# Token groups of two chunks behind the first, one v scaling moved ahead of other loads, and mix before score in the natural stops of a retention and snake kernel

## The chip, the cores and the metric

The kernel runs on one core of one Trainium2 chip. The metric is the device time of one execution in microseconds (us). Engines are named as the profile names them: PE is TensorE's matmul stream and PEld its weight loads, DVE is VectorE, ACT is ScalarE, POOL is GpSimd, SP is SyncE, which here only issues DMAs.

## The reference

Two layers follow each other. The first is a retention recurrence over 4 sequences of 768 tokens, with 8 heads of 64; its output, 3072 tokens of 512, goes into a feed-forward layer with a snake activation.

```python
for t in range(S):
    state = gamma[None, :, None, None] * state + np.einsum('bhd,bhe->bhde', k[:, :, t], v[:, :, t])
    y[:, :, t] = scale * np.einsum('bhd,bhde->bhe', q[:, :, t], state)
...
h = x @ w_in                                  # x: 3072 x 512, w_in: 512 x 2048
s = np.sin(alpha * h)
g = h + s * s / (alpha + 1e-09)
return (g @ w_out).astype(np.float32)         # w_out: 2048 x 512
```

## The kernel before

**Chunks and groups.** Each sequence is cut into six chunks of 128 tokens, 24 in all (`NJ`). The list `order`, also called `P`, holds first the four chunks 0 of the four sequences (`e0` to `e3`) and then, sequence by sequence, the chunks 1 to 5: `P[4]` to `P[8]` are of sequence 0, `P[9]` to `P[13]` of sequence 1, `P[14]` to `P[18]` of sequence 2, `P[19]` to `P[23]` of sequence 3. The list `sizes` (L49) cuts `P` into token groups for the feed-forward layer: 4, 2, 2, 2, 3, 3, 4, 4 chunks. Groups are numbered from 0.

**Attention of a chunk** has two parts. The score part multiplies keys with queries into PSUM (`pa`); DVE masks this into `aT`. The mix part multiplies `aT` with the scaled values and the state `s_bd` with the queries into `py`; DVE scales this into the chunk's columns of `xT`, the input of the feed-forward layer. It also adds keys times values of the chunk to the state, and casts of ACT, or of POOL for the last sequence, hand the state on as `s_bd` (L286, L391). Chunks of sequence 0 and `P[9]` take the natural form, `stage_A` for the score and `stage_M` for the mix. All later chunks are "wide" (L86) and take `scores`, `inter` and `mix`, which `burst` (L398) issues at one stop: state part of the old chunk, score of the new one, mix of the old one. DVE's and ACT's part of a burst follows at the next slot ("exit", "keep", "hand").

**Values and keys.** POOL issues all the loads that cast to bf16: `load_chunk` (L83, one DMA each for q, k and v of a chunk) and `load_seq` (L103, eight DMAs, one per head, for q, k or v of the wide chunks of a sequence). `scale_v` (L137) multiplies a chunk's values by a decay table on POOL, between these DMA issues, in program order. Queries and keys of a chunk are turned by DMA transposes that SP issues in order (`turn`, L256), or on PE at the start (`stage_T`).

**The feed-forward layer of a group** is a phase (L543). A phase goes through the 16 blocks of `d_ff`. `nf` blocks make a slot: 1 for groups of three and four chunks, 2 for groups of two, so that a slot has 512 columns of PSUM at most. In a slot PE makes `ph` (L425, four matmuls per block over all columns of the group), ACT takes the sine of each block (L428), squares the slot (L433; in the slots listed in `on_vector` DVE squares it, L435), and DVE adds (L440) into `gT`. While the phase of group g runs, PE also makes the output `po` of group g-1 (L450, 16 matmuls of 512 columns per chunk), spread over the slots; ACT copies a finished `po` to `o_sb` (L462) and SP stores it (L463). After the last phase PE makes the outputs of the last group with nothing beside them, the last chunk's in three column pieces (`last_tile`, L465).

**PSUM.** `ph` and `po` share the four buffers of tag "mm". A new `ph` waits until the buffer's last user is read: the adds of an earlier slot, or the copy of a finished `po`.

**Where attention stands.** `where` (L708 to L713) gives for each n the phase and slot after whose `ph` the stop for `P[n]` is made: there `P[n]` is scored and `P[n-1]` is mixed, the DMA transpose of `P[n+2]` is issued, and from n = 19 on `P[n]`'s values are scaled. All chunks of group g+1 must be mixed in the phase of group g. In a natural stop the score of `P[n]` is issued first and the mix of `P[n-1]` after it (L736 to L740).

**The start.** Group 0 is done by hand, up to L707, beside the weight loads. The loads of L670 to L697 are POOL's stream from then on.

Of the kernel before, what the change touches and what calls it, by code (L numbers as in the profile page):

```python
# [15 lines left out]
def kernel(  # L16
# [15 lines left out]
    nc = tc.nc  # L32
# [13 lines left out]

    order = [b * NCH for b in range(B)]
    order += [b * NCH + c for b in range(B) for c in range(1, NCH)]
    sizes = [4, 2, 2, 2, 3, 3, 4, 4]  # L49
    assert sum(sizes) == NJ  # L50
    NG = len(sizes)
    groups = [order[sum(sizes[:g]):sum(sizes[:g + 1])] for g in range(NG)]
# [16 lines left out]
    def chunk_of(t, j):  # L69
        b, c = divmod(j, NCH)  # L70
        return t[b, :, c * C:(c + 1) * C, :].rearrange("h s d -> s h d")

    def load_chunk(j, names="qkv"):
        for name, src in (("q", q), ("k", k), ("v", v)):
            if name not in names:
                continue
            if name == "v":
                t = big.tile([128, H, D], BF16, name="vr", tag="vr", bufs=10)
            else:
                if ("qk", j) not in raw:  # L80
                    raw["qk", j] = big.tile([128, 2, H, D], BF16, name="qkr", tag="qkr", bufs=9)
                t = raw["qk", j][:, "qk".index(name)]
            nc.gpsimd.dma_start(out=t, in_=chunk_of(src, j))  # L83
            raw[name, j] = t

    def wide(j):  # L86
        return j >= NCH + 2 and j % NCH > 0

    def load_seq(bt, names="qkv"):

        cs = [c for c in range(NCH) if wide(bt * NCH + c)]
        nh = 2 * len(cs)
        if "q" in names:
            raw["seq", bt] = (big.tile([128, nh, 2, NP, D], BF16, name=f"qk_seq{bt}"),
                              big.tile([128, nh, NP, D], BF16, name=f"v_seq{bt}"))
        tqk, tv = raw["seq", bt]
        for name, src in (("q", q), ("k", k), ("v", v)):
            if name not in names:
                continue
            for h in range(H):  # L100
                r = slice(64 * (h // NP), 64 * (h // NP) + 64)
                o = tv[r, :, h % NP, :] if name == "v" else tqk[r, :, "qk".index(name), h % NP, :]
                nc.gpsimd.dma_start(out=o, in_=src[bt, h, cs[0] * C:, :].rearrange("(f i) d -> i f d", i=64))  # L103
        for i, c in enumerate(cs):
            j, f = bt * NCH + c, slice(2 * i, 2 * i + 2)
            raw["qk", j], raw["k", j], raw["v", j] = tqk[:, f], tqk[:, f, 1], tv[:, f]
# [26 lines left out]
    def scale_v(j, eng):  # L133
        t, by = raw["v", j], kg
        if wide(j):
            t, by = t.rearrange("i f p d -> i (f p) d"), kgq
        eng.tensor_mul(t, t, by[:, j % NCH, :, None].to_broadcast([128, H, D]))  # L137
# [265 lines left out]
    def run(more, *kinds):  # L403
        for kind in kinds:
            if more and kind in more:
                more.pop(kind)()
# [40 lines left out]
    def ff_out(g, ts, f):  # L447
        if (g, ts) not in po:
            po[g, ts] = psum.tile([128, d_model], F32, name="po", tag="mm", bufs=4)
        nc.tensor.matmul(po[g, ts], gT[g][:, f, ts * C:(ts + 1) * C], w_out[:, f, :],  # L450
                         start=(f == 0), stop=(f == FF - 1))
        if f == FF - 1:
            take(g, ts)
# [29 lines left out]
    def out_pieces(g, tss):  # L483
        return [lambda ts=ts, f=f: ff_out(g, ts, f) for ts in tss for f in range(FF)]
# [58 lines left out]
    def phase(g, outs, att, nf=1, on_vector=()):  # L543


        no, done = len(outs), 0
        for n in range(FF // nf):
            more, fresh = rest[0], {}
            now = Slot(g, n * nf, nf=nf).sq("D" if n in on_vector else "A")
            run(more, "exit", "keep", "hand")  # L550
            for fn in att.get(n, ()):
                fresh.update(fn() or {})
            run(fresh, "mask")
            if fresh:
                rest[0] = fresh
            now.add()
            while done < no * (n + 1) * nf // FF:
                outs[done]()
                done += 1
# [4 lines left out]
    def X(j):  # L564
        return lambda: turn(j)
# [7 lines left out]
    def SK(j):  # L573
        return lambda: keep_S(j, stage_S(j))
# [3 lines left out]
    P = order  # L578
# [11 lines left out]
    def fill(n):  # L590
        for _ in range(n):
            outs.pop(0)()
# [81 lines left out]
    load_seq(1, "q")  # L674
    load_chunk(P[8], "v")
    scale_v(P[7], nc.gpsimd)
    load_seq(1, "k")
    load_chunk(P[9], "v")
    scale_v(P[8], nc.gpsimd)
    scale_v(e1, nc.gpsimd)  # L680
    load_seq(1, "v")
    scale_v(e2, nc.gpsimd)
    load_seq(2, "q")
    for j in P[9:12]:
        scale_v(j, nc.gpsimd)
    load_seq(2, "k")
    for j in P[12:14]:
# [17 lines left out]
    fill(4)  # L705
    stage_M(P[5])
    fill(4)  # L707
    where = {6: (1, 1), 7: (1, 3), 8: (1, 5)}  # L708
    for g in range(2, NG - 1):
        first = P.index(groups[g + 1][0])  # L710
        slots = {(2, 2): (2, 6), (2, 3): (0, 3, 6), (3, 3): (2, 7, 12)}.get((sizes[g], sizes[g + 1]), (2, 6, 10, 14))
        for i, n in enumerate(slots):
            where[first + i + 1] = (g, n)  # L713
    atts = {g: {} for g in range(1, NG)}

    def at(place, fn):
        atts[place[0]].setdefault(place[1], []).append(fn)
# [8 lines left out]
    def B(old, new, first):  # L726
        return lambda: burst(old, new, first)

    at((1, 0), T(P[7]))
    for n in range(6, NJ + 1):  # L730
        new = P[n] if n < NJ else None
        first = new - 1 if n < NJ and new % NCH == 1 else None
        if n > 6 and wide(P[n - 1]):
            at(where[n], B(P[n - 1], new, first))
        else:
            at(where[n], lambda j=new: (scores if wide(j) else stage_A)(j))  # L736
            if n > 6:
                at(where[n], lambda j=P[n - 1], last=wide(new): (M_last if last else stage_M)(j))
            if first is not None:
                at(where[n], SK(first))  # L740
        if n + 2 < NJ:
            at(where[n], X(P[n + 2]))
        if n >= 19 and n < NJ:
            at(where[n], lambda j=new: scale_v(j, nc.gpsimd))
    phase(1, outs, atts[1], 2, (2, 5))
    for g in range(2, NG):
        phase(g, out_pieces(g - 1, range(sizes[g - 1])), atts[g], 1 if sizes[g] > 2 else 2,
              (5, 10, 15) if sizes[g] == 3 and sizes[g - 1] == 2 else ())
    for fn in out_pieces(NG - 1, range(sizes[-1] - 1)):
        fn()  # L750
    last_tile(NG - 1, sizes[-1] - 1)
# [28 lines left out]
```

## Time and profile before

| | us |
|---|---|
| median of 3 runs | 224.99 |
| the runs | 227.31, 224.36, 224.99 |
| time of the profiled execution | 226.16 |
| span of the profiled execution, first to last instruction | 224.3 |

| engine | busy us | share of the span | instructions |
|---|---|---|---|
| PE | 207.0 | 92% | 2005 |
| PEld | 116.2 | 52% | 2005 |
| ACT | 163.1 | 73% | 322 |
| DVE | 140.8 | 63% | 285 |
| POOL | 107.1 | 48% | 145 |

Matmuls are pipelined, so one that is listed with 279 ns follows the one before it after a shorter time; the spacing of starts is what a stage is counted by. The first `ph` of phase 2 starts at 63.19 us, of phase 3 at 84.94, of phase 4 at 101.62, of phase 5 at 125.74, of phase 6 at 151.83 and of phase 7 at 179.63; the first output matmul with no phase beside it follows at 207.25. POOL issues loads until about 119 us. The mean granted clock of TensorE is 0.992.

### The profile page before, as it was taken

To read this page: it belongs to the slowest core of one execution; us is meant where nothing else is said; L and a number is where in the kernel's file an instruction comes from. 1 tells how busy PE (TensorE), PEld (TensorE's weight loads), DVE (VectorE), ACT (ScalarE), POOL (GpSimd) and SP (SyncE) were. 2 spreads that over 40 slices of the span, in tenths; PEclk is the share of its full clock that TensorE was granted. 3 is DMA by queue.
4 is the path that set the end of the run, shared out by engine and by line. 5 is a ranking of instruction groups with operands and counts; after the bars stand their busy time and mean duration, and the time that the engine had idled before them with its cause. 6 is when DMAs were issued, how large, how long until landed. Compare 5 with 4: busy or idle time off the path is not lost.

```text
span 224.3 us, 5046 instructions
## 1 busy us (share of the span) xinstructions
PE 207.0 (92%) x2005; PEld 116.2 (52%) x2005; DVE 140.8 (63%) x285; ACT 163.1 (73%) x322; POOL 107.1 (48%) x145
## 2 busy tenths in 40 slices
PE   7798999899999679999879899999999999999994
PEld 3444544466666446775445455555455444444454
DVE  4887769958977346665797676766677543443100
ACT  7679697757698727979858977869778788787221
POOL 8965346995599899899992100033321000000000
PEclk9999999999999979999999999999999999999999
DMA  9999999999999999999999124133011011101212
GB/s 129 148 190 192 207 206 158 154 143 222 151 95 195 167 85 146 109 153 170 189 165 123 43 53 106 37 96 94 1 51 47 3 47 47 47 3 47 93 47 94
DMA packets 101334, 24.96 MB, mean 111 GB/s; under 512 B 93872, under 2 KB 98368, under 8 KB 101312
## 3 DMA queue, kind: packets, MB, share of 16 engines
q0 software_dynamic: 77504, 13.38, 84.5%
q1 hardware_dynamic: 23664, 11.22, 23.8%
q8 instruction: 15, 0.25, 0.5%
q10 hardware_dynamic: 144, 0.07, 0.1%
q14 instruction: 7, 0.06, 0.1%
HBM read 27.27 MB, written 6.29 MB: 150 GB/s over the span
## 4 chain that ended last, share of the span: by engine, by line
PE 49%; DMA 20%; POOL 15%; DVE 7%; ACT 7%; issue 2%; POOLq 0%; DVEq 0%
PE po L450 23%; PE ph L425 20%; DMA w_out<-in_moe_w_out_dram 7%; DMA w_in<-in_moe_w_in_dram 4%; DMA qk_seq<-in_q_dram 4%; DMA qkr<-in_k_dram 4%; POOL qkr L83 4%; POOL qk_seq L103 3%; DVE gT L440 3%; ACT s L428 2%; POOL vr L83 2%; POOL v_seq L103 2%; ACT s L433 2%; POOL vr L137 2%; ACT s_bd L391 2%
## 5 line engine op out<-in xcount | busy, mean ns | idle before, releaser
L440 DVE SCALAR_TENSOR_TENSOR gT<-s,rec_alpha,ph 128x256 bf16<-128x256 f32 (+3 forms) x136 | 76.5, 587 | 53.9 <-ACT s L433 53.6
L425 PE MATMUL ph<-xT,w_in 128*128 128x256 bf16 (+3 forms) x544 | 100.3, 318 | 4.3 <-DVE gT L440 4.2
L450 PE MATMUL po<-w_out,gT 128*128 128x512 bf16 x368 | 97.5, 382 | 1.1 <-DVE gT L440 0.7
L428 ACT ACTIVATE s<-ph,alpha_sb 128x256 f32<-128x256 f32 (+3 forms) x136 | 72.5, 559 | 30.4 <-PE ph L425 28.9
L425 PEld LDWEIGHTS <-w_in 128*128 128x128 bf16 x544 | 52.2, 99 | 46.6 <-issue 7.9
L433 ACT ACTIVATE s<-s 128x512 f32<-128x512 f32 (+1 forms) x97 | 57.2, 590 | 2.7
L450 PEld LDWEIGHTS <-gT 128*128 128x128 bf16 x368 | 34.2, 98 | 34.1 <-issue 2.1
L391 POOL CAST s_bd<-s_f 64x256 bf16<-64x256 f32 x10 | 3.9, 394 | 41.0 <-DVE s_f L386 21.5
L462 ACT COPY o_sb<-po 128x512 f32<-128x512 f32 x23 | 13.2, 578 | 9.3 <-PE po L450 9.0
L103 POOL DMA_DIRECT2D qk_seq<-in_q_dram x24 | 17.1, 744 | 3.2 <-DMA qkr<-in_k_dram 2.4
L103 POOL DMA_DIRECT2D qk_seq<-in_k_dram x24 | 17.0, 744 | 2.5 <-DMA qk_seq<-in_q_dram 2.4
L103 POOL DMA_DIRECT2D v_seq<-in_v_dram x24 | 17.1, 764 | 0.8 <-DMA qk_seq<-in_k_dram 0.8
L137 POOL TENSOR_TENSOR v_seq<-v_seq,kgq 128x512 bf16<-128x512 bf16 x14 | 14.7, 1098 | 4.8 <-DMA v_seq<-in_v_dram 4.4
L346 DVE TENSOR_TENSOR aTw<-pa,maskq 128x768 bf16<-128x768 f32 x14 | 13.3, 953 | 1.3 <-PE pa L341 1.0
L492 PE MATMUL spare<-warm 128*128 128x512 bf16 x28 | 9.9, 480 | 1.2 <-DVE warm L156 1.2
L83 POOL DMA_DIRECT2D vr<-in_v_dram x10 | 9.2, 922 | 3.2 <-DMA w_in<-in_moe_w_in_dram 1.6
L377 DVE TENSOR_TENSOR xT<-py,qg 128x256 bf16<-128x256 f32 x28 | 10.5, 415 | 0.0
L83 POOL DMA_DIRECT2D qkr<-in_k_dram x9 | 8.1, 900 | 4.0 <-DMA w_out<-in_moe_w_out_dram 3.4
L83 POOL DMA_DIRECT2D qkr<-in_q_dram x9 | 8.1, 898 | 3.7 <-DMA w_in<-in_moe_w_in_dram 1.7
L286 ACT CAST s_bd<-ps 64x256 bf16<-64x256 f32 x14 | 5.1, 364 | 6.4 <-PE ps L279 6.3
L435 DVE TENSOR_TENSOR s<-s 128x512 f32<-128x512 f32 (+1 forms) x9 | 8.9, 990 | 0.3 <-ACT s L428 0.3
L303 PE MATMUL py<-aT,vr 128*64 128x128 bf16 x80 | 4.0, 221 | 5.0 <-POOL vr L137 3.8
(92 smaller groups left out, 158.0 us busy)
## 6 DMA issues: line engine op xcount, KB each, us to landing
out_dram<-o_sb SPq DMA_DIRECT2D x23, 256.0 KB, 2.2
w_in<-in_moe_w_in_dram POOLq DMA_DIRECT2D x4, 512.0 KB, 11.0
w_out<-in_moe_w_out_dram POOLq DMA_DIRECT2D x4, 512.0 KB, 14.8
vr<-in_v_dram POOLq DMA_DIRECT2D x10, 128.0 KB, 7.0
qk_seq<-in_q_dram POOLq DMA_DIRECT2D x16, 80.0 KB, 5.4
qk_seq<-in_k_dram POOLq DMA_DIRECT2D x16, 80.0 KB, 5.4
v_seq<-in_v_dram POOLq DMA_DIRECT2D x16, 80.0 KB, 5.4
qkr<-in_q_dram POOLq DMA_DIRECT2D x9, 128.0 KB, 7.1
```

What stands on the lines that cost most here:

```text
L83: nc.gpsimd.dma_start(out=t, in_=chunk_of(src, j))
L103: nc.gpsimd.dma_start(out=o, in_=src[bt, h, cs[0] * C:, :].rearrange("(f i) d -> i f d", i=64))
L137: eng.tensor_mul(t, t, by[:, j % NCH, :, None].to_broadcast([128, H, D]))
L346: return {"mask": lambda: nc.vector.tensor_mul(aT, pa[:, :, 0:384].rearrange("p e (m t) -> p e m t", m=2), maskq[:, None, None, :].to_broa ...
L377: nc.vector.tensor_mul(x[:, 2 * b:2 * b + 2, :], py[b][:, 0:256].rearrange("p (m t) -> p m t", m=2), qg[:, c, 2 * b:2 * b + 2])
L425: nc.tensor.matmul(self.ph[:, m, :], w_in[:, i, f * 128:(f + 1) * 128], xT[g][:, i, self.lo:self.hi], start=(m == 0 and i == 0), stop=(i = ...
L428: nc.scalar.activation(out=self.s[:, m, :], in_=self.ph[:, m, :], func=ACTF.Sin, scale=alpha_sb[:, f:f + 1])
L433: nc.scalar.activation(out=self.s, in_=self.s, func=ACTF.Square)
L440: nc.vector.scalar_tensor_tensor(gT[self.g][:, f, self.lo:self.hi], self.s[:, m, :], rec_alpha[:, f:f + 1], self.ph[:, m, :], op0=ALU.mult ...
L450: nc.tensor.matmul(po[g, ts], gT[g][:, f, ts * C:(ts + 1) * C], w_out[:, f, :], start=(f == 0), stop=(f == FF - 1))
L462: nc.scalar.copy(o_sb, po[g, ts])
L492: nc.tensor.matmul(spare["ps"], warm[:, :128], warm, start=True, stop=True)
```

## The change

`sizes` becomes one group of four and ten groups of two, so all phases have `nf` = 2 and eight slots. Stops are at slots 1 and 5 of every phase from 2 on, where there were two to four stops at slots that depended on the sizes; the stop for `P[8]` goes from slot 5 of phase 1 to slot 6. DVE squares no slot any more in the phases behind phase 1. On POOL, the load of `P[9]`'s values goes ahead of the k load of sequence 1, and their scaling from behind the q load of sequence 2 to ahead of the v load of sequence 1. In the natural stops the mix of the old chunk comes before the score of the new one. With the sizes, the group to which each chunk belongs moves too: `P[10]` and `P[11]` make group 4, and the last group is `P[22]` and `P[23]`.

```diff
-    sizes = [4, 2, 2, 2, 3, 3, 4, 4]
+    sizes = [4] + [2] * 10
...
     load_seq(1, "q")
     load_chunk(P[8], "v")
     scale_v(P[7], nc.gpsimd)
+    load_chunk(P[9], "v")
     load_seq(1, "k")
-    load_chunk(P[9], "v")
     scale_v(P[8], nc.gpsimd)
     scale_v(e1, nc.gpsimd)
+    scale_v(P[9], nc.gpsimd)
     load_seq(1, "v")
     scale_v(e2, nc.gpsimd)
     load_seq(2, "q")
-    for j in P[9:12]:
+    for j in P[10:12]:
         scale_v(j, nc.gpsimd)
...
-    where = {6: (1, 1), 7: (1, 3), 8: (1, 5)}
+    where = {6: (1, 1), 7: (1, 3), 8: (1, 6)}
     for g in range(2, NG - 1):
         first = P.index(groups[g + 1][0])
-        slots = {(2, 2): (2, 6), (2, 3): (0, 3, 6), (3, 3): (2, 7, 12)}.get((sizes[g], sizes[g + 1]), (2, 6, 10, 14))
-        for i, n in enumerate(slots):
+        for i, n in enumerate((1, 5)):
             where[first + i + 1] = (g, n)
...
         else:
-            at(where[n], lambda j=new: (scores if wide(j) else stage_A)(j))
             if n > 6:
                 at(where[n], lambda j=P[n - 1], last=wide(new): (M_last if last else stage_M)(j))
+            at(where[n], lambda j=new: (scores if wide(j) else stage_A)(j))
...
-        phase(g, out_pieces(g - 1, range(sizes[g - 1])), atts[g], 1 if sizes[g] > 2 else 2,
-              (5, 10, 15) if sizes[g] == 3 and sizes[g - 1] == 2 else ())
+        phase(g, out_pieces(g - 1, range(sizes[g - 1])), atts[g], 2)
```

## The prediction

> **What bounds the kernel now.** The chain of waits (PE 49%, DMA 20%, POOL 15% of the span) mixes two regimes, so I cut the span at the first `ph` of each phase and asked for busy times by stretch. Columns: stretch, length, busy time of PE, PEld, DVE, ACT, POOL with instruction counts, granted clock, DMA share, GB/s.
>
> ```profile
> 63.19:84.94 21.75, 17.98 (x168) 11.67 (x168) 11.23 (x23) 14.61 (x32) 20.93 (x28) 0.92 1.61 135
> 84.94:101.62 16.68, 16.68 (x254) 11.75 (x253) 12.12 (x29) 13.36 (x30) 15.90 (x22) 1.00 2.02 140
> 101.62:125.74 24.12, 21.01 (x246) 11.77 (x245) 18.05 (x36) 19.17 (x39) 18.79 (x24) 1.00 1.77 145
> 125.74:151.83 26.09, 24.91 (x314) 14.11 (x313) 18.11 (x37) 20.72 (x41) 1.83 (x3) 1.00 0.30 72
> 151.83:179.63 27.80, 27.74 (x290) 13.75 (x288) 18.29 (x36) 22.20 (x36) 6.28 (x11) 1.00 0.13 39
> 179.63:207.25 27.62, 27.62 (x129) 12.54 (x128) 12.17 (x17) 22.79 (x37) 0.00 (x0) 1.00 0.10 39
> 207.25:224.30 17.05, 14.06 (x97) 8.01 (x95) 1.04 (x2) 3.52 (x8) 0.00 (x0) 1.00 0.21 77
> ```
>
> These are phases 2 to 7 and the tail. Phases 3, 6 and 7 are all PE; phases 2, 4 and 5 are not, and phase 2 lost clock as well. PE's timeline in phases 2 and 3 shows why (start, length, what; in brackets idle time before it and who ended it):
>
> ```profile
> 76.00 0.41 PE L299 MATMUL py<-qkT,s_bd 128*64 128x128 bf16 x8
> 80.18 0.41 PE L303 MATMUL py<-aT,vr 128*64 128x128 bf16 x8 [3.77 <-POOL vr L137]
> 80.43 0.29 PE L279 MATMUL ps<-vr,qkr 128*64 128x64 bf16 x8
> 80.65 1.12 PE L450 MATMUL po<-w_out,gT 128*128 128x512 bf16 x4
> 81.57 1.91 PE L425 MATMUL ph<-xT,w_in 128*128 128x256 bf16 x8
> 83.27 1.83 PE L450 MATMUL po<-w_out,gT 128*128 128x512 bf16 x4
> ...
> 87.61 1.04 PE L425 MATMUL ph<-xT,w_in 128*128 128x256 bf16 x8
> 88.48 1.03 PE L450 MATMUL po<-w_out,gT 128*128 128x512 bf16 x4
> 89.34 1.04 PE L425 MATMUL ph<-xT,w_in 128*128 128x256 bf16 x8
> ```
>
> The mix of `P[9]` waits 3.77 us for its scaled values. After that eight `ph` matmuls take 83.27-81.57 = 1.70 us instead of 88.48-87.61 = 0.87, and the four `po` 1.67 instead of 0.86: the slow clock costs 1.6 us more. POOL's timeline says why the values are late:
>
> ```profile
> 63.15 0.91 POOL L83 DMA_DIRECT2D vr<-in_v_dram  x1
> 64.07 2.06 POOL L137 TENSOR_TENSOR vr<-vr,kg 128x512 bf16<-128x512 bf16 x2
> 66.06 5.48 POOL L103 DMA_DIRECT2D v_seq<-in_v_dram  x8
> 71.47 1.14 POOL L137 TENSOR_TENSOR vr<-vr,kg 128x512 bf16<-128x512 bf16 x1
> 72.46 2.22 POOL L103 DMA_DIRECT2D qk_seq<-in_q_dram  x3
> 75.48 3.58 POOL L103 DMA_DIRECT2D qk_seq<-in_q_dram  x5 [0.81 <-issue]
> 79.02 1.11 POOL L137 TENSOR_TENSOR vr<-vr,kg 128x512 bf16<-128x512 bf16 x1
> ```
>
> The last line scales `P[9]`; it stands behind sixteen load issues. In phases 4 and 5 PE waits for DVE's adds instead (all such waits of the page: total, times, longest):
>
> ```profile
> PE ph L425 <- DVE gT L440: 4.2, 8, 0.9
> ```
>
> **The change, part by part.** The plan of the sum: what PE must do from 63.19 on, before and after, then the new waits.
>
> *PE's work in a phase of twos.* A slot is 89.34-87.61 = 1.735 us (eight `ph` 0.87, four `po` 0.865), a burst 0.92 (PE 85.81 to 86.73), a natural stop with its state part 1.02 (67.63 to 68.65). Check: 8 x 1.735 + 3 x 0.92 = 16.64, and phase 3 took 16.68. Afterwards: phase 2 is 13.88 + 2 x 1.02 = 15.9; phases 3 to 9 are 13.88 + 2 x 0.92 = 15.72 each, 110.0 in all; phase 10, without stops, is 13.88. The tail has 16 `po` for the first chunk of the last group (3.46), the last tile (3.55) and what lies behind PE's end (221.32 to 224.3, 3.0): 10.0. Sum 149.8, so the span would end at 63.19 + 149.8 = 213.0.
>
> *The same count for before.* Phases 4 to 7 from 0.65 for four 384-column `ph`, 0.86 for four 512-column ones and 0.216 per `po`: 20.1, 24.45, 27.9, 27.7; with 15.9, 16.64 and the tail's 17.05, 149.7. It took 161.1. So PE's work stays, and what the change can win is the 11.4 us of holes: 5.85 in phase 2, 4.0 in phase 4 (20.1 of work in 24.1), 1.6 in phase 5.
>
> *Smaller groups on PE.* Groups of three and four had 128 `ph` at 384 and 128 at 512 columns; seven groups of two have 448 at 256, so 192 matmuls and weight loads more. By the rows 128 x 0.1625 + 128 x 0.2155 = 48.4 us become 448 x 0.1085 = 48.6. The weight loads (99 ns each) lie under the matmuls: the pace per column is the same for the three widths. [...] The rows here are 216 ns at 512 and 108 at 256, in proportion, so the sum goes by them.
>
> *ACT and DVE.* A slot of two blocks costs ACT 1.40 us in stream (sine at 97.05 to the next slot's at 98.45), a hand-over 0.83, an output copy 0.59: 8 x 1.40 + 2 x 0.83 + 2 x 0.59 = 14.0 of a phase's 15.72; without stops 12.4 of 13.88. DVE: 8 x 0.87 for adds, 2 x 0.95 for masks, 2 x (0.74 + 0.47) for exits and state, 11.3. In all ACT's sines get dearer (112 x 469 ns instead of 32 x 577 + 32 x 688, +12 us), and PE hides that: in phase 3, with a stop more, ACT's share was as high (14.8 of 16.68) and PE never waited. If this cover went, each us of ACT above 15.7 per phase would cost seven. [...]
>
> *DVE squares.* Phase 4 squared three slots on DVE (2.5 us for the first one); those and the sixteen narrow slots with 1.08 us of PE against 1.03 of ACT made its holes. They go; a slot of twos has 1.735 against 1.40.
>
> *`P[9]`'s values.* The scaling moves ahead of eight issues of v of sequence 1 and eight of q of sequence 2. That removes 3.77 + 1.6 us and the rest of phase 2's loss. What is late next? The load of `P[9]`'s v is now ahead of the k loads; it is two of these in size, and they run at 1.0 us each (57.25, 58.24, 59.22), waiting for earlier loads to land. So k of sequence 1 and everything on POOL up to the three scalings come 0 to 2 us later. Scaled `P[8]`, `e1` and `P[10]` were ready at 65.1, 66.1 and 81.1; they are now needed at 66.05 (slot 1 of phase 2, a slot earlier than before), 66.6 and 82.2 (slot 1 of phase 3): waits of 0 to 1.6 in all. The DMA transpose of `P[10]` went out at 65.73, when k was there; out at 65.7 to 67.7 and landing 3.7 later (its own row) to 9.7 (the slowest of all transposes), against a need at 74.4: 0 to 3. On SP the stores of outputs queue behind it; three `o_sb` buffers and one copy per 8 us cover that. I take 0.5 for all of this, bounds 0 and 3.2: at the median landing of 6.3 even the late transpose is there at 74.0, and a shift of 1 us leaves the scalings 0.5 late at most.
>
> *Mix before score, stop at slot 6.* The score of `P[8]` waited 0.55 us for its transpose at 58.64; a slot later this is gone. DVE gets the exit before the 1.22 us mask. Against it, `xT` of phase 2 is finished a slot later, with one slot (1.3 us) left: -0.6 to +0.5, I take 0. In the other natural stops the 0.7 us mix covers late transposes.
>
> *Phase starts.* Phases 2 and 4 began with waits on adds of 0.32 and 0.55; phase 3 with none. Eight starts at 0 to 0.55: 0 to 4.4, I take 0.5, nearest to phase 3, which has the new shape on both sides. The tail needs the last adds: 0.84 + 0.63 + 0.87 after the last `ph`, under 18 `po` (3.9): 0, at most 1. Exits now have a slot to spare, and sequences 2 and 3 are needed later than before.
>
> Sum: 213.0 + 0.5 + 0.5 = 214.0 as the span, 10.3 less than 224.3. The profiled execution took 226.16, 1.86 over its span and 1.17 over the median; the median less 10.3 is 214.7. I predict **215**.
>
> **The rivals.** *Weight loads exposed (slower).* At the `ph` of phases 4 to 10, 192 more loads of 98 ns cost 18.8 us if nothing hides them: 224.3 - 10.3 + 18.8, about 233 against the median. It decides above 54 ns per load. For: every second matmul now reloads for half the columns. Against: phases 1 to 3 load so already at 108 ns per matmul. Chance 0.05.
>
> *The adds keep PE waiting.* If every phase of twos pays 0.55 at its start or at the buffer behind an output copy, 4.4 us come back; at 0.92, the longest, 7.4: 219 to 222. For: eight such waits in before, one at 63.19 in a phase of twos. Against: none inside phases 2 and 3. Chance 0.15.
>
> *The supply stall moves.* `P[9]`'s wait returns at `P[10]` or at its transpose, up to 3.2 and 1.6 of slow clock, or the scaling isn't early enough and 5.4 stay: 218 to 220. For: POOL has no idle time in phase 2 (20.93 of 21.75). Against: the moved scaling is some 12 us early for its mix at slot 5. Chance 0.10.
>
> **How the numbers follow.** The forecast has 0.70. Its own range is 212.5 (no new wait, 0.6 gained in phase 1, half a us of run noise) to 217.5. With the better half of the middle rivals the 8-in-10 range is 212.5 to 219.5. Against no change, about 2% (220.5 and 229.5) can be told: faster takes the forecast and most of the two middle rivals, 0.86; within 2% 0.08; slower 0.06, the first rival.
>
> **What would show it.** In the changed profile: no wait of PE on POOL's L137 above 1 us; clock 1.00 through phase 2; `ph` at 0.87 per eight to the end; phase starts 15.7 us apart; PE's waits on L440 under 1 us in all; ACT about 14 us busy in each phase. It is wrong if PE idles at the transposes of `P[10]` to `P[12]`, if phases are longer than 16 us with ACT full, or if weight loads open gaps between matmuls.

## The result and the profile after

| | before | after |
|---|---|---|
| median, us | 225.19 (4 runs, 224.36 to 227.31) | 216.34 (4 runs, 215.39 to 216.94) |
| ratio after / before | | 0.9589, 95% interval 0.9515 to 0.9664 |
| profiled execution: time, span | 226.16, 224.3 | 216.35, 214.6 |
| PE busy in the span | 207.0 (92%) | 202.1 (94%) |
| ACT busy | 163.1 (73%) | 167.6 (78%) |

The change made the kernel 4.1% faster. Forecast were 215 us and a span of 214.0. Some runs of a kernel are more than 1.5% longer than its fastest one; the medians in the next section leave them out.

The stretches of the changed kernel, cut at the first `ph` of each phase from 2 to 10, and the tail; columns as in the prediction:

```profile
62.37:78.93 16.56, 16.08 (x168) 11.01 (x168) 11.55 (x24) 14.16 (x32) 14.78 (x21) 1.00 1.64 131
78.93:95.36 16.43, 15.73 (x199) 11.01 (x200) 10.63 (x27) 13.29 (x30) 15.72 (x21) 1.00 2.02 161
95.36:111.44 16.08, 15.76 (x192) 10.99 (x193) 10.64 (x27) 13.67 (x31) 16.08 (x22) 1.00 1.84 166
111.44:127.39 15.95, 15.63 (x199) 10.94 (x200) 10.63 (x27) 13.66 (x31) 9.60 (x13) 1.00 1.22 127
127.39:143.35 15.96, 15.64 (x199) 10.95 (x200) 10.63 (x27) 13.64 (x31) 0.00 (x0) 1.00 0.27 67
143.35:159.35 16.00, 15.68 (x191) 11.01 (x192) 10.64 (x27) 12.90 (x28) 3.17 (x6) 1.00 0.39 69
159.35:175.10 15.75, 15.43 (x200) 10.95 (x200) 10.63 (x27) 12.50 (x27) 3.59 (x7) 1.00 0.18 51
175.10:190.55 15.45, 15.13 (x168) 10.61 (x169) 9.47 (x24) 12.49 (x27) 1.34 (x3) 1.00 0.10 37
190.55:204.44 13.89, 13.79 (x95) 9.40 (x96) 6.98 (x17) 12.49 (x27) 0.00 (x0) 1.00 0.10 39
204.44:214.60 10.16, 7.15 (x65) 4.90 (x63) 1.17 (x4) 2.50 (x6) 0.00 (x0) 1.00 0.22 78
```

Phases 2 to 8 take 15.8 to 16.6 us, close to the 15.72 that the prediction counted for the matmuls of a phase with two bursts, and the granted clock is 1.00 in every stretch. Phase 9 is shorter because its last stop has no new chunk to score. (PE's busy time is some 0.3 short of most stretches because one `po` record is missing behind most stops, 344 of 368 in the page; the next start is where it belongs, so there is no hole.)

PE's timeline at the mixes of `P[9]` and `P[10]`, the second wait being the only one on POOL that is left:

```profile
73.59 0.41 PE L299 MATMUL py<-qkT,s_bd 128*64 128x128 bf16 x8
73.84 0.39 PE L303 MATMUL py<-aT,vr 128*64 128x128 bf16 x8
...
82.61 0.25 PE L354 MATMUL py<-aTw,v_seq 64*64 64x128 bf16 x4 [0.39 <-POOL v_seq L137]
```

And POOL's timeline, where three scalings, the third of them `P[9]`'s, end at 67.05, and `P[10]`'s begins at 81.50:

```profile
64.01 3.04 POOL L137 TENSOR_TENSOR vr<-vr,kg 128x512 bf16<-128x512 bf16 x3
67.00 5.48 POOL L103 DMA_DIRECT2D v_seq<-in_v_dram  x8
...
81.50 2.05 POOL L137 TENSOR_TENSOR v_seq<-v_seq,kgq 128x512 bf16<-128x512 bf16 x2
```

Of the 4.2 us of `ph` waits on DVE's adds one wait is left, at 31.6 us, ahead of phase 1 (total, times, longest):

```profile
PE ph L425 <- DVE gT L440: 0.2, 1, 0.2
```

From phase 2 on no `ph` waits for the adds for more than 0.1 us; only an output matmul does, for 0.17 us in the first slot of phase 2.

### The profile page after: what moved, and what is told of

It reads as the page before. It is cut to its first block, busy times and chain, and to the rows that moved or that the text cites. A ratio compares the mean times of both kernels' runs of the same rounds, so it can differ in the third digit from the quotient of the medians.

```text
span 214.6 us, 5482 instructions
## 1 busy us (share of the span) xinstructions
PE 202.1 (94%) x2171; PEld 134.5 (63%) x2197; DVE 141.4 (66%) x330; ACT 167.6 (78%) x365; POOL 107.2 (50%) x145
## 4 chain that ended last, share of the span: by engine, by line
PE 59%; DMA 25%; POOL 12%; issue 2%; DVE 0%; POOLq 0%; DVEq 0%
PE po L450 27%; PE ph L425 26%; DMA w_out<-in_moe_w_out_dram 8%; DMA w_in<-in_moe_w_in_dram 5%; DMA v_seq<-in_v_dram 4%; POOL qkr L83 4%; DMA qk_seq<-in_q_dram 4%; DMA qkr<-in_k_dram 4%; POOL v_seq L103 2%; POOL vr L83 2%; PE poh L473 2%; POOL vr L137 1%; PE py L327 1%; PE pa L337 1%; POOL qk_seq L103 1%
## 5 line engine op out<-in xcount | busy, mean ns | idle before, releaser
L440 DVE SCALAR_TENSOR_TENSOR gT<-s,rec_alpha,ph 128x256 bf16<-128x256 f32 (+3 forms) x184 | 82.2, 488 | 55.1 <-ACT s L433 54.7
L428 ACT ACTIVATE s<-ph,alpha_sb 128x256 f32<-128x256 f32 (+3 forms) x184 | 79.2, 480 | 28.8 <-PE ph L425 27.6
L425 PE MATMUL ph<-xT,w_in 128*128 128x256 bf16 (+3 forms) x735 | 98.6, 277 | 0.3 <-DVE gT L440 0.2
L450 PE MATMUL po<-w_out,gT 128*128 128x512 bf16 x344 | 90.3, 379 | 3.9 <-issue 3.2
L425 PEld LDWEIGHTS <-w_in 128*128 128x128 bf16 x736 | 70.5, 98 | 31.8 <-issue 2.8
L269 DVE TENSOR_TENSOR aT<-pa,mask 128x1024 bf16<-128x1024 f32 x6 | 7.3, 1217 | 0.7 <-PE pa L265 0.7
L137 POOL TENSOR_TENSOR vr<-vr,kg 128x512 bf16<-128x512 bf16 x7 | 7.5, 1091 | 0.1
```

The source lines that it names most:

```text
L425: nc.tensor.matmul(self.ph[:, m, :], w_in[:, i, f * 128:(f + 1) * 128], xT[g][:, i, self.lo:self.hi], start=(m == 0 and i == 0), stop=(i = ...
L428: nc.scalar.activation(out=self.s[:, m, :], in_=self.ph[:, m, :], func=ACTF.Sin, scale=alpha_sb[:, f:f + 1])
L440: nc.vector.scalar_tensor_tensor(gT[self.g][:, f, self.lo:self.hi], self.s[:, m, :], rec_alpha[:, f:f + 1], self.ph[:, m, :], op0=ALU.mult ...
```

## The experiments

All times are medians; each group of runs has its own runs of the kernel before beside it (medians of 224.6 to 226.2 us). The ratios are those on record, with their 95% intervals.

**The moved values alone** (`vmove`), and the changed kernel without them (`no_vmove`). The edit, put on the kernel before and taken from the changed one:

```diff
+    load_chunk(P[9], "v")
     load_seq(1, "k")
-    load_chunk(P[9], "v")
     scale_v(P[8], nc.gpsimd)
     scale_v(e1, nc.gpsimd)
+    scale_v(P[9], nc.gpsimd)
...
-    for j in P[9:12]:
+    for j in P[10:12]:
```

> The kernel before with the load and the scaling of P[9]'s values moved, and nothing else. Theory (the late scaling costs phase 2 its wait and its clock, and POOL gets later behind it): the 3.77 us wait and the 1.6 us of slow clock go; the mix of P[10], at slot 0 of phase 3, is reached at about 80.4 us while its scaling ends at about 82.5, so about 2 us come back there. 225.2 - 5.8 + 2.1 = 221.5 us. Rival (the stall only moves on): 224 to 225. Rival (the move alone is most of the gain): 217 to 218.

> The changed kernel with the load and the scaling of P[9]'s values back at their old places. Theory: its mix at slot 5 of phase 2, about 73.8 us, waits until about 80.2, 6.3 us, the clock falls for 1.6 us more, and the 0.4 us wait at P[10] goes: 216.3 + 7.4 = 223.7 us. Rival (with the stops at 1 and 5 the place of the scaling does not matter): 216 to 217.

`vmove` took 219.79 us, ratio 0.9729 (0.9637 to 0.9821). Its phase 2 fell from 21.75 to 16.11 us, at a granted clock of 1.00 instead of 0.92, and phase 3 rose from 16.68 to 18.02, with a wait of 1.15 us at `P[10]`. The mechanism is the theory's, but the time lies between its 221.5 us and the 217 to 218 of the rival that gave the move most of the gain: the wait behind it was half of what I allowed. `no_vmove` took 224.63 us, ratio 0.9999 (0.9948 to 1.0049): by the medians, without the moved values the other edits win nothing. PE's timeline of `no_vmove`:

```profile
73.67 0.41 PE L299 MATMUL py<-qkT,s_bd 128*64 128x128 bf16 x8
79.31 0.64 PE L303 MATMUL py<-aT,vr 128*64 128x128 bf16 x8 [5.23 <-POOL vr L137]
...
82.24 1.91 PE L425 MATMUL ph<-xT,w_in 128*128 128x256 bf16 x8
83.95 1.59 PE L450 MATMUL po<-w_out,gT 128*128 128x512 bf16 x4
```

With the stop at slot 5 the mix is reached at 73.7 instead of 76.0 us and POOL is only 0.9 us earlier, so the wait is 5.23 us instead of 3.77, and the clock falls: eight `ph` take 1.71 us behind the wait (82.24 to 83.95) and 0.87 again from 85.38 on, and the mean granted clock of the execution is 0.983 where it was 0.992. Phase 2 takes 24.5 us here and 21.75 in the kernel before, so the old POOL order costs 2.8 us more under the new stops. In this plan the move is worth 8.3 us by the medians (224.63 against 216.34) and 7.6 us by the spans of the two profiles; on the kernel before it is 4.9 (224.64 beside `vmove`) and 6.2. The profiled execution of `no_vmove` is 2.1 us shorter in span than the one of before, so that the other edits win nothing at all without the move holds for the medians and not for each run (222.99 to 226.43 us).

**The old sizes with all the rest** (`threes`), the same with ACT squaring (`threes_act`), and with the stops of phase 3 later (`threes_late`). The first is the changed kernel with the sizes, and with them the stops and DVE's squares behind phase 1, as before; the second and the third change one line of the first each:

```diff
-    sizes = [4] + [2] * 10
+    sizes = [4, 2, 2, 2, 3, 3, 4, 4]
...
-              (5, 10, 15) if sizes[g] == 3 and sizes[g - 1] == 2 else ())
+              ())
...
-        slots = {(2, 2): (2, 6), (2, 3): (0, 3, 6), (3, 3): (2, 7, 12)}.get((sizes[g], sizes[g + 1]), (2, 6, 10, 14))
+        slots = {(2, 2): (2, 6), (2, 3): (1, 4, 6), (3, 3): (2, 7, 12)}.get((sizes[g], sizes[g + 1]), (2, 6, 10, 14))
```

> The changed kernel with the old group sizes, stops and DVE squares behind phase 1 (the score order, the stop at slot 6 of phase 1 and the moved values stay as changed). Theory: 0.8 us less than the kernel before with the moved values alone, which is about 220.7 us; phases 4 and 5 keep holes of 4.0 and 1.6 us. Rival (the holes came from what the late start of phase 3 left behind): they shrink to under 2 us together, 217 us.

> As threes, but in phase 4 ACT squares the three slots too that DVE squared. Theory (ACT's 1.03 us per slot, three hand-overs and two copies fill PE's 20.1 us, so PE waits either way): phase 4 stays above 22.5 us, the time within 1.5 us of threes. Rival (the squares on DVE, 2.5 us for the first one, made the hole): phase 4 falls to about 20.5 us and the time by 3.5 us.

> As threes, but the three stops of phase 3 at slots 1, 4 and 6 instead of 0, 3 and 6. It tells apart what the sizes win: the holes of the groups of three, or the later stop of P[10]. Theory (both): the wait of P[10] falls from 2.4 us to under 1 and phase 3 to under 18.5 us; phases 4 and 5 keep 3.5 to 4.5 us of holes over the 44.6 us of their work; 218.5 to 219.5 us. Rival (the holes alone): 220.0 as threes. Rival (the later stop alone): 216.5 to 217.

`threes` took 220.00 us, ratio 0.9742 (0.9655 to 0.9828), 3.7 above the changed kernel and not the 0.8 below `vmove` that the theory had. No run of the four kernels with the old sizes and the move is under 219.0 us, and none of the changed kernel is over 216.94. The profiled execution of `threes` is its longest, 221.97 us: phase 3 takes 20.83 us there, with a wait of 2.35 at `P[10]` and a clock of 0.92. Its phases 4 and 5 in the windows view:

```profile
99.46:121.61 22.15, 20.69 (x246) 11.77 (x245) 16.15 (x36) 19.18 (x39) 20.53 (x27) 1.00 2.09 160
121.61:147.69 26.08, 24.90 (x313) 14.12 (x312) 18.09 (x37) 20.71 (x41) 2.87 (x4) 1.00 0.40 78
```

They take 48.2 us for the 44.55 of matmuls that the prediction counted: 3.7 us of holes. `threes_act` took 219.98 us (0.9725, 0.9637 to 0.9812), with 22.55 and 26.70 us for the two phases in the profile of its longest run, at a clock of 1.00 in both: the holes are there without any square on DVE behind phase 1. The prediction's other cause, slots of 1.08 us of PE over a phase that is as full on ACT, fits `threes_act`: 16 x 1.03 + 3 x 0.82 + 2 x 0.58 = 20.1 us of ACT for 20.1 of PE. It isn't shown. In `threes` three of the sixteen slots have no square on ACT, so ACT needs less, and the holes of phase 4 are nearly as large (2.05 us against 2.45); of these, 1.45 are waits of `ph` on DVE's adds. What makes the adds late in groups of three stays open.

`threes_late` took 220.92 us (0.9760, 0.9686 to 0.9834), above the 218.5 to 219.5 of the theory. In its profile the wait of `P[10]` is gone and phase 3 takes 17.51 us, but phases 4 and 5 take 23.70 and 26.73 us, 5.9 of holes, more than I expected; DVE's squares can explain a part of that (last section). So the run doesn't part the two causes: the holes grew while the stop moved. How much of the 3.7 us is the later stop of `P[10]` and how much the holes stays open.

**ACT's room** (`act1`, `act2`). One idle copy in each slot behind phase 1, and two in `act2`:

```diff
             now = Slot(g, n * nf, nf=nf).sq("D" if n in on_vector else "A")
+            if g > 1:
+                for _ in range(1):
+                    nc.scalar.copy(tiny, warm[:, 0:1])
```

> The changed kernel with one extra copy of a single column on ACT (about 0.2 us) behind the square of every slot of phases 2 to 10; its result is not used. Theory (a phase of twos has 15.7 us of PE over 14.0 of ACT, so ACT has 1.7 to give): ACT rises by 8 x 0.2 = 1.6 per phase and still fits; waits at the buffers grow a little: 216.3 to 218 us. Rival (ACT is already what paces the phases of twos): 72 x 0.2 = 14 us more, 230 us.

> As act1 with two extra copies in every slot. Theory: ACT needs 14.0 + 3.2 = 17.2 us in phases 2 to 6, 1.5 more than PE, fits in phases 7 to 9 (12.4 + 3.2 = 15.6) and needs 1.7 more than PE in phase 10: 7.5 + 1.7 = 9.2, so 225.5 us. Rival (ACT paces already): 28 us more, 244. Rival (ACT's work is hidden by more than this, the phases are not near a limit): under 219.

`act1` took 217.48 us, `act2` 221.45: 1.1 and 5.1 above the changed kernel. `act1` is as forecast, `act2` 4 us under its 225.5. The rival that ACT paces already falls. A pair of copies lengthens ACT's slot from 1.40 to 1.71 us (sine at 106.74 to the next one at 108.45 in `act2`), so by 0.31 and not by 0.40. With that price the theory's count by phases gives 5.0 us (0.8 in each of phases 2 to 6, 1.0 in phase 10), as measured, but by luck, for the loss lies elsewhere: phases 4 to 6 take 17.2 to 17.3 us, 1.3 more than in the changed kernel, phase 7 takes 0.6 more, phases 3 and 10 take 0.3 more, and phases 2, 8 and 9 lose nothing. PE's waits in `act2` show where ACT meets PE:

```profile
PE ph L425 <- ACT o_sb L462: 4.6, 8, 0.6
```

It is eight waits of 0.6 us, from slot 5 of phase 3 to slot 1 of phase 7, and not the adds but the copy of a finished `po` ends them. This copy stands behind a hand-over and a slot's work on ACT, and the next `ph` takes its buffer. In `act1` the same eight places wait 0.13 to 0.15 us each. So ACT never runs out over a phase (it is busy for 15.9 of the 17.3 us of phase 4 in `act2`); it is late where a hand-over, a slot and a copy follow each other, and the room there is less than the 1.7 us of the whole phase.

**Two groups of four at the end** (`fours_end`).

```diff
-    sizes = [4] + [2] * 10
+    sizes = [4, 2, 2, 2, 2, 2, 2, 4, 4]
...
-        for i, n in enumerate((1, 5)):
+        slots = {(2, 2): (1, 5), (2, 4): (0, 2, 4, 6)}.get((sizes[g], sizes[g + 1]), (2, 6, 10, 14))
+        for i, n in enumerate(slots):
```

> The changed kernel with the last eight chunks as two groups of four: sizes 4, 2 x 6, 4, 4; four stops in the eight slots of phase 6 and four in the sixteen of phase 7. Theory (PE's work is the same for every width, only slots where PE's share is near ACT's open holes): phase 8 as full of PE as phase 7 of the kernel before; phase 7, with 1.30 us of PE and about 1.28 of ACT per slot, opens holes of 1 to 3 us: 217.5 to 219 us. Rival (twos are faster in themselves): 220 and more. Rival (width makes no difference anywhere behind the loads): 216.3, within half a us.

It took 218.44 us (0.9680, 0.9613 to 0.9748), in the theory's range for the wrong reason. Phase 7 runs from 146.26 to 171.16, 24.9 us for 24.45 of work: less than half a us of holes, where the theory had 1 to 3. The loss is in phase 6, 19.9 us for 13.88 + 4 x 0.92 = 17.6, where PE waits for the states handed over (1.2 us on ACT's casts, 0.4 on POOL's); four stops stand only two slots apart there. So the groups of four cost little in themselves, and counting ACT by the slot (1.28 of 1.30) was too coarse: phase 7 hands over on POOL.

**The natural stops as before** (`old_stops`).

```diff
+            at(where[n], lambda j=new: (scores if wide(j) else stage_A)(j))
             if n > 6:
                 at(where[n], lambda j=P[n - 1], last=wide(new): (M_last if last else stage_M)(j))
-            at(where[n], lambda j=new: (scores if wide(j) else stage_A)(j))
...
-    where = {6: (1, 1), 7: (1, 3), 8: (1, 6)}
+    where = {6: (1, 1), 7: (1, 3), 8: (1, 5)}
```

> The changed kernel with the score ahead of the mix again in the natural stops, and P[8]'s stop back at slot 5 of phase 1. Theory: worth 0 to 0.8 us (phase 1 took 14.92 us before and 14.11 after; the kernel before with the moved values alone took 14.28, and 219.8 us against 220.0 with the stops changed too): 216.3 to 217.1. Rival (the order hides the late transposes of P[9] and P[10], which wait without it): 1.5 us more and above, with PE waits on the DMA that writes qkT.

215.80 us (0.9586, 0.9502 to 0.9670): the same as the changed kernel. The only wait on a transpose in its profile, 0.6 us, is at the score of `P[6]`, a stop that the edit doesn't touch.

**Trying to beat it** (`early_scale`, `hand_pool`, `both`).

```diff
-    load_seq(2, "q")
     for j in P[10:12]:
         scale_v(j, nc.gpsimd)
+    load_seq(2, "q")
...
-                copy = nc.gpsimd.tensor_copy if now // NCH == 3 else nc.scalar.copy
+                copy = nc.gpsimd.tensor_copy if now >= 15 else nc.scalar.copy
```

> The changed kernel with the scalings of P[10] and P[11] ahead of the q load of sequence 2 on POOL. Theory: P[10] is scaled by about 78.5 us instead of 82.5, the 0.4 us wait of its mix goes; POOL waits for v of sequence 1 to land, so the loads of sequence 2 come up to 4 us later, which their slack of 10 us and more takes: 0.4 us less than the changed kernel, and no run with a slow clock in phase 3. Rival (the loads of sequence 2 become late): PE waits on the transposes of P[14] at about 106 us, slower.

> The changed kernel with the state casts of P[16] to P[18] on POOL, which has no loads left by then, instead of ACT. Theory (slots 1 and 5 are 0.11 us longer while ACT hands over, because the copy of a finished output stands behind it on ACT and the next ph takes that buffer): these two slots fall to 1.735 us in phases 6 and 7, about 0.4 us in all. Rival (the 0.11 us has another cause): no change in the slots.

> early_scale and hand_pool together: 0.8 us less than the changed kernel by the two theories, 215.5 us; at most 0.2 less if neither holds.

215.90 (0.9571, 0.9532 to 0.9609), 215.47 (0.9558, 0.9522 to 0.9594) and 216.04 us (0.9577, 0.9541 to 0.9613): none can be told from the changed kernel. In `early_scale` `P[10]` is scaled from 76.19 us on instead of 81.50 and its mix doesn't wait, but it waits as little in `hand_pool`, `old_stops` and `fours_end`, which leave that scaling where it was: phase 3 takes 15.85 or 15.86 us in all four. The 0.39 us are thus a chance of the profiled execution, and nothing is won by the edit. One further run of `early_scale` took 220.57 us at a mean clock of 0.992, so that no run would have a slow clock isn't borne out. The mechanism of `hand_pool` does show: the slots behind a hand-over on POOL are 1.74 us, where the changed kernel's are 1.84 and 1.87, and phases 6 and 7 take 15.88 and 15.87 instead of 15.96 and 16.00. That is 0.2 us where 0.4 was expected. Some tenths of a microsecond are less than the runs differ by.

## Why the prediction was right

**The end and the terms.** Each term, as forecast and as measured in the profile after, in us:

| term | forecast | measured |
|---|---|---|
| start of phase 2 | 63.19 | 62.37 |
| phase 2 | 15.9 | 16.56 |
| phases 3 to 9 | 110.0 | 111.62 |
| phase 10 | 13.88 | 13.89 |
| tail | 10.0 | 10.16 |
| waits put on top | 1.0 | in the rows above |
| span | 214.0 | 214.60 |

The main reasoning, that PE's work stays and the holes go, is what the runs show: the 11.4 us above the count of PE's work became 2.4. That the span came within 0.6 us of the forecast is partly luck. The phases and the tail took 2.4 us more than their count where 1.0 was allowed, and phase 2 started 0.82 us earlier than counted, for which the forecast had no reason: phase 1 takes 14.11 to 14.92 us in the profiles of seven of these kernels.

**`P[9]`'s values.** The mechanism is shown by `vmove` and `no_vmove`. What the prediction didn't say is that the edits depend on each other: the earlier stops make the old POOL order 2.8 us dearer in phase 2, and in the medians this eats what the other edits win. What was late next came as bounded: the three scalings started at 64.01 and `P[10]`'s at 81.50 instead of 80.02, within the 0 to 2 us, and cost 0.39 us of wait in this profile. The transposes of `P[9]` to `P[12]` cost nothing.

**Smaller groups on PE.** Right: 640 matmuls of 256 columns keep 0.87 us per eight to the end, with 192 weight loads (98 ns each) more. The rival of exposed loads falls. Matmuls of 256 columns stand 108 ns apart in this stream, as forecast.

**ACT and DVE.** Right that PE hides them; that a phase's sum says how much room ACT has is wrong, as `act2` shows. The 12 us more of sines are a sum of durations. Sines of a slot overlap in part (184 with a mean of 480 ns would be 88.3 us), and the busy time of their line rose from 72.5 to 79.2 us, that of all of ACT by 4.5 in a span that is 9.7 us shorter.

**The holes of threes.** The forecast was 5.6 us for phases 4 and 5; with the move made, the four profiles with the old sizes have 3.7 to 5.9 us of holes there, and their kernels are 3.5 to 4.6 us above the changed one. That the new sizes, with the stops that go with them, remove the holes is shown. The causes that the prediction gave for them are not: `threes_act` keeps the holes without the squares, and ACT's share is argued.

**Sizes that were off.** A natural stop costs 1.25 and 1.11 us at slots 1 and 5 of phase 2 (from 2.98 and 2.84 us slots, less 1.735), not 1.02; the slot in the kernel before that the 1.02 was read from, 66.66 to 69.52, already gives 1.13 in this way. The wait on the adds at the starts of phases, taken at 0.5 us together, shows in the first slot of phase 2 alone, with 0.33 (2.06 us, less 1.735). The rival of waits at the buffer behind an output copy is there, at a fifth of its price: while ACT hands over, the `ph` of slots 1 and 5 start 0.11 us late, eight times from slot 5 of phase 3 to slot 1 of phase 7. On ACT the hand-over comes ahead, and the copy ends at 96.59 + 0.57 = 97.16, when the next `ph` starts (PE, 97.20). ACT's timeline of the changed kernel there:

```profile
94.37 0.80 ACT L391 CAST s_bd<-s_f 64x256 bf16<-64x256 f32 x2
95.18 0.84 ACT L428 ACTIVATE s<-ph,alpha_sb 128x256 f32<-128x256 f32 x2
96.05 0.63 ACT L433 ACTIVATE s<-s 128x512 f32<-128x512 f32 x1
96.59 0.57 ACT L462 COPY o_sb<-po 128x512 f32<-128x512 f32 x1
```

**The natural stops.** I took 0 within -0.6 and +0.5, and phase 1 came out 0.8 us shorter. `old_stops` shows that the order and the stop are worth nothing measurable, so the 0.8 is a chance of the two profiled executions: the 0.55 us that `P[8]`'s score waited for its transpose in before are absent from `vmove` and `old_stops` too, which have the stop at the same slot and the score ahead of the mix.

## What to carry to other kernels

Count the bound engine's work for each stage before and after; if it is the same, a change can win the holes and no more, and each hole has to be named by who ended it. An in-order queue that mixes loads and small compute steps is a timetable: ask when the consumer arrives after the change, because a consumer that comes earlier makes an unmoved step dearer (a wait of 5.23 us in `no_vmove` instead of 3.77). For a second engine neither a sum over the stage nor a count by the slot is enough (`act2` and `fours_end` each missed by one of them): look for the place where its steps follow each other without a pause and the bound engine needs the last of them. A wait of some tenths of a microsecond in one profile can be chance: see whether it is there in the profiles of kernels that leave that place alone.

## What the runs showed of the hardware

DVE's square of a slot takes 0.55 us at 384 columns, and 2.0 to 2.7 when it meets POOL's scalings. DVE in the kernel before:

```profile
111.63 2.53 DVE L435 TENSOR_TENSOR s<-s 128x384 f32<-128x384 f32 x1
...
120.35 0.55 DVE L435 TENSOR_TENSOR s<-s 128x384 f32<-128x384 f32 x1
```

and POOL in the kernel before:

```profile
111.58 2.15 POOL L137 TENSOR_TENSOR v_seq<-v_seq,kgq 128x512 bf16<-128x512 bf16 x2
```

The slow one lies within 0.5 us of POOL's two scalings at both ends; the other, with no scaling beside it, is fast. It is the same in `vmove` (2.03 us at 112.68, scalings from 112.22 to 114.28) and `threes_late` (2.74 at 112.67, scalings from 112.93 to 114.99). In `threes` no square meets a scaling and all three take 0.55 us; phase 4 takes 22.15 us there and 22.99 to 24.12 in the three others. In phase 1, whose squares have 512 columns, chance makes the comparison. In before and `no_vmove` DVE's first square there meets a scaling and takes 1.86 and 1.68 us; in the changed kernel, `vmove`, `threes` and `threes_late` it is over before the scaling starts and takes 0.69. In `no_vmove` a `ph` waits 0.58 us for the adds some 3 us later; in the other five none in phase 1 does.

In all five overlaps the square ends a fixed time behind POOL's scalings, wherever it began: 0.42 or 0.43 us with 384 columns and 0.56 with 512, a little less than the 0.55 and 0.69 that it takes alone. So the square as good as waits for the end of the scalings, two in a row in phase 4. Which of the two records starts first makes no difference to that: in three of the five it is the square's, by 0.06 to 0.26 us (53.96 against 54.21 in phase 1 of before), and it is still the square that is late. What holds DVE up the profile doesn't show. No run was made to change the overlap, so its share of the holes of phase 4 is read from these profiles and not shown by an experiment.
